# Agent attention with two layers: the last three token tiles are 416, 416 and 384 columns wide in place of 512, 512 and 192

## The chip, the cores and the metric

The kernel runs on one core of one Trainium2 chip. The metric is the device time of one execution in microseconds (us), as the median over runs. The engines of a core work side by side, each through its own queue in order: PE (TensorE) multiplies matrices, DVE (VectorE) and ACT (ScalarE) do elementwise work, POOL (GpSimd) does elementwise work on SBUF, and SP issues transfers. PE writes its results to PSUM, from which DVE and ACT read.

## The reference, cut to what matters

```python
a2k = sm(agents, k);  agent_v = a2k @ v      # softmax over 12480 keys, 49 agents
q2a = sm(q, agents);  x = q2a @ agent_v      # 12480 tokens x 128
h = x @ w_in;   g = h * (1 / (1 + exp(-h)));  x = g @ w_out     # layer 1, 2048 hidden
h = x @ w2_in;  g = h * cos(h);               out = g @ w2_out  # layer 2, 2048 hidden
```

The inputs are q, k, v (12480 x 128 each), the agents (49 x 128) and two pairs of weights. The output is 12480 x 128.

## The kernel before

The attention comes first: it leaves the softmax weights of all 12480 tokens in SBUF as `pT`, tokens along the free axis, and folds `agent_v` into the first layer's weights. It takes about the first tenth of the time and doesn't know the token tiles of the layers.

The layers run over 25 **tiles** of tokens, 24 of 512 and a last one of 192. `toks(t)` is a tile's width and `span(t)` its slice of tokens. The 2048 hidden units are cut into 16 chunks of 128. A **group** g is a quarter of a tile (`t = g // 4`, `m = g % 4`): four chunks, handled as two pairs k = 0, 1. There are NG = 100 groups. Values are split in a high part in a short format and a low part, the rest, so that three matmuls give one product; the letters h and l at the end of names say which part (`g2h`, `g2l`).

Layer 1 of a group: `L1_rest` and `L1_h` multiply into two pairs of PSUM banks (lines 543 and 555), `L1_act` applies Silu on ACT (563), `L1_hi` casts on ACT (570), `L1_lo` subtracts on DVE (578), and `L1_y` adds the product with the second weights into one bank, y1 (587, 588, 591). At a tile's end `L1_end_a` and `L1_end_b` make layer 2's input, `x2h` on ACT (608) and `x2l` on DVE (616).

Layer 2 of a group: `L2_h` (PE, 629 to 631, six matmuls a pair) gives h; `L2_n` on ACT (643) rounds h to a number of turns, `L2_r` on DVE (653) takes the turns away, `L2_cos` on ACT (662), `L2_g` on DVE (670) multiplies with h and with that frees the PSUM pair; `L2_hi` casts (679, on DVE, for some last pairs on ACT), `L2_lo` subtracts on POOL (688; the very last pair on DVE), and `L2_y` (again 587, 588, 591) adds into the one bank y2. At a tile's end `L2_end` transposes y2 on DVE (710), which frees the bank, and SP sends four transfers to the output (712).

Pairs of PSUM banks come from a pool of three (`ps`). Layer 2 runs LAG = 5 groups behind layer 1: iteration g of the last loop does layer 1 of group g and layer 2 of group q = g - 5. Up to iteration 99 the code's order is the order of each engine's queue (`manual_schedule`). At g == NG that ends (`steady.close()`): from there, where layer 1 has no more groups, a scheduler orders the queues. In the last group (`parts`) elementwise work is cut into single chunks.

Of the kernel before, what the change touches and what calls it, by code (L numbers as in the profile page):

```python
# [26 lines left out]
NWARM = 9  # L27
LATER = 150
WIDE = 512
LAG = 5  # L30
SUP = 960
LINE = 32
# [3 lines left out]
def agent_attention_moe_moe_kernel(ctx, tc, q, k, v, agents, w_in, w_out, w2_in, w2_out, out):  # L36
    nc = tc.nc
    _, N, C = q.shape
# [36 lines left out]
    def b32(ap):  # L75
        return ap.bitcast(F32)
# [367 lines left out]
    with ExitStack() as ml:  # L444
        def pool(name, bufs):
            return ml.enter_context(tc.tile_pool(name=name, bufs=bufs))
# [9 lines left out]
        g2h_p = pool("g2h", 3)  # L456
        g2l_p = pool("g2l", 3)
        o_p = pool("o", 2)
        NL = (N + WIDE - 1) // WIDE
        NG = NL * 4  # L460
        pTf = pT.rearrange("a t p s -> a (t p s)")

        def toks(t):
            return min(WIDE, N - t * WIDE)

        def span(t):
            return slice(t * WIDE, t * WIDE + toks(t))

        o1h, o1l = split["o1"]
        i2h, i2l = split["i2"]  # L470
# [8 lines left out]
        def wide(pool, tag, dt, g):  # L479
            return pool.tile([128, 2, WIDE], dt, tag=tag, name=tag)[:, :, :toks(g // 4)]  # L480

# [6 lines left out]

        avh, avl = (g1l_p.tile([128, 2, WIDE], F32R, tag="g1l", name=nm)[:, 0, :256] for nm in ("avh", "avl"))
        v.tensor_copy(out=avh, in_=pn)  # L490
# [29 lines left out]
        def in_place_low(y, cs):  # L520
            v.tensor_tensor(out=w2h[96:128, cs], in0=y[96:128], in1=b32(w2l)[96:128, cs], op=ALU.subtract)


        def L1_rest_in(t):
            if not 0 <= t < NL:
                return
            x = x3_p.tile([128, WIDE], F32R, tag="x3", name="x3")[:, :toks(t)]
            src = b32(pTf)[MORE:NA, span(t)]
            for i in range(4):
                nc.sync.dma_start(out=b32(x)[32 * i:32 * i + REST, :], in_=src)  # L530
            x3s[t] = x
# [16 lines left out]
        def L1_h(g, k):  # L548
            if not 0 <= g < NG:
                return  # L550
            t, m = g // 4, g % 4
            x = pTf[:, span(t)]
            for j in range(2):
                c = 4 * m + 2 * k + j
                nc.tensor.matmul(  # L555
                    out=h1s[g, k][:, j, :toks(t)], lhsT=w2h[:, 128 * c:128 * c + 128], rhs=x, start=False, stop=True
                )
# [35 lines left out]
        def L1_y(g, k):  # L593
            if not 0 <= g < NG:
                return
            t, m = g // 4, g % 4
            if m == 0 and k == 0:
                y1s[t] = banky("y1")[:, :toks(t)]
            gh, gl = g1s.pop((g, k))
            three(y1s[t], o1h, o1l, gh, gl, 4 * m + 2 * k)  # L600
# [34 lines left out]
        def parts(g):  # L635
            return [slice(0, 1), slice(1, 2)] if g == NG - 1 else [slice(0, 2)]
# [36 lines left out]
        def L2_hi(g, k):  # L673
# [4 lines left out]
            for p in parts(g):  # L678
                (sc.copy if k and g + LAG >= NG else v.tensor_copy)(out=gh[:, p], in_=g2s[g, k][0][:, p])  # L679
            g2s[g, k].append(gh)  # L680
# [24 lines left out]
        def L2_end(g):  # L705
            if not (0 <= g < NG and g % 4 == 3):
                return
            t = g // 4
            o = o_p.tile([128, WIDE // 32, 32], F32, tag="o", name="o")[:, :toks(t) // 32]
            v.transpose(out=o.rearrange("p b j -> p (b j)"), in_=y2s.pop(t))  # L710
            for cb in range(4):
                nc.sync.dma_start(
                    out=out[span(t), 32 * cb:32 * cb + 32].rearrange("(b i) j -> i b j", i=32),
                    in_=o[32 * cb:32 * cb + 32],
                )
# [19 lines left out]
        in_place_low(a2, q2)  # L735
        for g in range(LAG):

# [15 lines left out]
            if g == 1:  # L753
                in_place(a3, q3)
                in_place_low(a3, q3)
        for g in range(LAG, NG + LAG + 3):
            if g == NG:
                steady.close()
            q = g - LAG
            if g % 4 == 1:  # L760
# [4 lines left out]
            L1_h(g, 0)  # L765
            if g == LAG:
                L1_y(g - 1, 0)
# [56 lines left out]
```

## Time and profile before

| What | Value |
|---|---|
| median of 3 runs | 1134.94 us (1134.33 to 1134.96) |
| the profiled execution, its own time | 1131.78 us |
| its span, first to last instruction | 1130.0 us |
| busy share of the span | PE 96%, PEld (weight loads) 75%, DVE 87%, ACT 82%, POOL 48% |
| mean granted clock of PE | 0.991 of full |

Busy shares are means over the whole span. A matmul's row shows its latency, and matmuls overlap, so the distance between the starts of two that follow each other, their pitch, is what one costs on a full queue.

### The profile page before, as it was taken

Reading aid. Unit: us, or ns where it says so; the run is one execution under the profiler, and the core shown is the slowest. Engines: PE = TensorE matmul, PEld = TensorE weight load, DVE = VectorE, ACT = ScalarE, POOL = GpSimd, SP = SyncE. Lnnn points to the kernel's source line nnn. Section 1 sums busy time; section 2 is a strip of 40 time slices with the busy share of each in tenths; the row PEclk is TensorE's granted clock in tenths of the full one; section 3 lists DMA queues with packets and bytes.
Section 4 is the critical chain, followed back from the end, with each engine's and each line's share of the span. In section 5 each row is a group of like instructions: output and inputs, shape, how many; then the busy total and the mean of one; then the engine's idle time right before and its main releaser. Section 6 shows DMA issues by size and latency. Waiting matters only on the chain.

```text
span 1130.0 us, 14466 instructions
## 1 busy us (share of the span) xinstructions
PE 1084.7 (96%) x5377; PEld 851.7 (75%) x5377; DVE 988.6 (87%) x1075; ACT 923.7 (82%) x980; POOL 545.0 (48%) x291
## 2 busy tenths in 40 slices
PE   7877899999999999999999999999999999999996
PEld 5866667777777777777777777777777777777775
DVE  4899769999999999999999999999999999999884
ACT  3677698888888888888888888888888888888764
POOL 2467603554444455554444555544444555544554
PEclk9999999999999999999999999999999999999998
DMA  8898500000000000000000000000000000000000
GB/s 234 216 228 199 114 9 6 3 13 16 13 3 15 15 10 6 15 15 1 16 15 11 5 16 16 1 15 15 13 3 15 16 8 8 15 13 1 10 10 13
DMA packets 76902, 38.69 MB, mean 34 GB/s; under 512 B 52483, under 2 KB 69184, under 8 KB 76832
## 3 DMA queue, kind: packets, MB, share of 16 engines
q1 hardware_dynamic: 76832, 37.78, 14.5%
q8 instruction: 42, 0.69, 0.3%
q14 instruction: 28, 0.23, 0.1%
HBM read 27.58 MB, written 6.39 MB: 30 GB/s over the span
## 4 chain that ended last, share of the span: by engine, by line
PE 80%; DVE 8%; ACT 4%; DMA 3%; issue 3%; POOL 1%; SPq 0%; DVEq 0%; ACTq 0%; POOLq 0%
PE y L587 15%; PE y L588 15%; PE y L591 15%; PE h L555 9%; PE h L629 8%; PE h L630 8%; PE h L631 8%; PE h L543 4%; DMA wraw<-in_moe_w_in_dram 2%; DVE g L670 1%; DMA wraw<-in_moe_w_out_dram 1%; ACT g L563 1%; DVE a L248 1%; DVE m L243 1%; ACT n L662 1%
## 5 line engine op out<-in xcount | busy, mean ns | idle before, releaser
L688 POOL TENSOR_TENSOR g2l<-g,g2h 128x1024 fp32r<-128x1024 f32 (+1 forms) x200 | 466.3, 2353 | 519.4 <-DVE g1l L578 496.1
L653 DVE SCALAR_TENSOR_TENSOR n<-n,h 128x1024 f32<-128x1024 int32 (+2 forms) x202 | 239.0, 1184 | 71.7 <-ACT n L643 58.5
L643 ACT ACTIVATE n<-h,quarter 128x1024 int32<-128x1024 f32 (+2 forms) x202 | 219.6, 1088 | 91.1 <-PE h L631 91.1
L578 DVE TENSOR_TENSOR g1l<-g,g1h 128x1024 fp32r<-128x1024 f32 (+1 forms) x200 | 239.8, 1199 | 16.9 <-ACT g1h L570 7.5
L670 DVE TENSOR_TENSOR g<-n,h 128x1024 f32<-128x1024 f32 (+2 forms) x202 | 238.0, 1179 | 7.0 <-ACT n L662 3.7
L662 ACT ACTIVATE n<-n,halfpi 128x1024 f32<-128x1024 f32 (+2 forms) x202 | 226.0, 1120 | 5.6 <-DVE n L653 5.6
L563 ACT ACTIVATE g<-h 128x1024 f32<-128x1024 f32 (+1 forms) x200 | 199.5, 997 | 37.5 <-PE h L555 37.4
L570 ACT CAST g1h<-g 128x1024 fp32r<-128x1024 f32 (+1 forms) x200 | 205.0, 1025 | 3.3
L679 DVE CAST g2h<-g 128x1024 fp32r<-128x1024 f32 (+1 forms) x196 | 154.8, 790 | 7.6 <-DVE g L670 0.5
L587 PE MATMUL y<-g2h,o2h 128*128 128x512 f32 (+1 forms) x400 | 155.9, 390 | 5.1 <-DVE o L710 3.4
L587 PE MATMUL y<-g1h,o1h 128*128 128x512 f32 (+1 forms) x400 | 156.3, 392 | 0.9 <-DVE x2l L616 0.5
L629 PE MATMUL h<-x2h,i2h 128*128 128x512 f32 (+1 forms) x400 | 154.8, 387 | 1.6 <-DVE g L670 1.6
L588 PE MATMUL y<-g2h,o2l 128*128 128x512 f32 (+1 forms) x400 | 155.5, 389 | 0.0
L631 PE MATMUL h<-x2l,i2h 128*128 128x512 f32 (+1 forms) x400 | 154.4, 386 | 0.9 <-DVE x2l L616 0.9
L630 PE MATMUL h<-x2h,i2l 128*128 128x512 f32 (+1 forms) x400 | 154.4, 386 | 0.0
L588 PE MATMUL y<-g1h,o1l 128*128 128x512 f32 (+1 forms) x400 | 153.6, 385 | 0.0
L555 PE MATMUL h<-pT,w2h 128*128 128x512 f32 (+1 forms) x400 | 132.7, 413 | 0.0
L591 PE MATMUL y<-g2l,o2h 128*128 128x512 f32 (+1 forms) x400 | 122.9, 388 | 0.2 <-POOL g2l L688 0.2
L591 PE MATMUL y<-g1l,o1h 128*128 128x512 f32 (+1 forms) x400 | 121.9, 386 | 0.1
L587 PEld LDWEIGHTS y<-g1h,o1h 128*128 128x128 f32 x400 | 75.1, 188 | 24.0 <-DVE x2l L616 8.4
L587 PEld LDWEIGHTS y<-g2h,o2h 128*128 128x128 f32 x400 | 76.1, 190 | 21.3 <-DVE o L710 3.6
L555 PEld LDWEIGHTS h<-pT,w2h 128*128 128x128 f32 x400 | 67.1, 188 | 31.6 <-issue 23.6
(129 smaller groups left out, 1200.1 us busy)
## 6 DMA issues: line engine op xcount, KB each, us to landing
raw<-in_q_dram SPq DMA_DIRECT2D x13, 480.0 KB
vraw<-in_v_dram SPq DMA_DIRECT2D x13, 480.0 KB
out_dram<-o SPq DMA_DIRECT2D x96, 64.0 KB
raw<-in_k_dram SPq DMA_DIRECT2D x12, 480.0 KB
wraw<-in_moe_w_in_dram SPq DMA_DIRECT2D x8, 512.0 KB
wraw<-in_moe_w_out_dram SPq DMA_DIRECT2D x8, 512.0 KB
x<-pT SPq DMA_DIRECT2D x96, 38.0 KB
raw<-in_k_dram SPq DMA_DIRECT2D x2, 240.0 KB
```

The source lines that it names most:

```text
L555: nc.tensor.matmul(out=h1s[g, k][:, j, :toks(t)], lhsT=w2h[:, 128 * c:128 * c + 128], rhs=x, start=False, stop=True)
L578: i = v.tensor_tensor(out=gl, in0=f, in1=b32(gh), op=ALU.subtract)
L587: nc.tensor.matmul(out=y, lhsT=wh[:, c, :], rhs=gh[:, j, :], start=(c == 0), stop=False)
L588: nc.tensor.matmul(out=y, lhsT=wl[:, c, :], rhs=gh[:, j, :], start=False, stop=False)
L591: nc.tensor.matmul(out=y, lhsT=wh[:, c, :], rhs=gl[:, j, :], start=False, stop=(c == NCH - 1))
L629: nc.tensor.matmul(out=y, lhsT=i2h[:, c, :], rhs=xh, start=True, stop=False)
L630: nc.tensor.matmul(out=y, lhsT=i2l[:, c, :], rhs=xh, start=False, stop=False)
L631: nc.tensor.matmul(out=y, lhsT=i2h[:, c, :], rhs=xl, start=False, stop=True)
L653: v.scalar_tensor_tensor(out=b32(n)[:, p], in0=n[:, p], scalar=-2.0 * PI, in1=h2s[g, k][:, p], op0=ALU.mult, op1=ALU.add)
L662: sc.activation(out=r[:, p], in_=r[:, p], func=AF.Sin, bias=halfpi)
L670: v.tensor_tensor(out=f[:, p], in0=r[:, p], in1=h[:, p], op=ALU.mult)
L688: i = (v if (g, k) == (NG - 1, 1) else gp).tensor_tensor(out=gl[:, p], in0=f[:, p], in1=b32(gh)[:, p], op=ALU.subtract)
```

## The change

The widths come from a list now: 22 tiles of 512, then 416, 416 and 384, which again are 12480 tokens in 25 tiles. Number of tiles, groups and instructions per group are the same. The first changed instruction is layer 1 of group 88.

```diff
+LAST = (416, 416, 384)
...
-        NL = (N + WIDE - 1) // WIDE
+        widths = [WIDE] * ((N - sum(LAST)) // WIDE) + list(LAST)
+        begins = [sum(widths[:i]) for i in range(len(widths))]
+        assert sum(widths) == N
+        NL = len(widths)
...
         def toks(t):
-            return min(WIDE, N - t * WIDE)
+            return widths[t]

         def span(t):
-            return slice(t * WIDE, t * WIDE + toks(t))
+            return slice(begins[t], begins[t] + widths[t])
```

Up to iteration 99 the queues hold the same instructions in the same order, with other widths. Behind it the scheduler orders them anew. Line numbers of the changed kernel are higher by four there (643 is 647, 653 is 657, 662 is 666, 670 is 674, 679 is 683, 710 is 714).

ACT's queue of the last tile, groups 96 to 98, before (643 is n, 662 the cosine, 679 the cast of a pair's high part):

```order
L679 CAST g2h<-g_9819 128x1024
L643 ACTIVATE n<-h,quarter 128x2x192
L662 ACTIVATE n<-n,halfpi 128x2x192
L643 ACTIVATE n<-h,quarter 128x2x192
L662 ACTIVATE n<-n,halfpi 128x2x192
L679 CAST g2h<-g_9865 128x2x192
L643 ACTIVATE n<-h,quarter 128x2x192
L662 ACTIVATE n<-n,halfpi 128x2x192
```

And of the change, the same place:

```order
L647 ACTIVATE n<-h,quarter 128x2x384
L683 CAST g2h<-g_9819 128x2x416
L647 ACTIVATE n<-h,quarter 128x2x384
L666 ACTIVATE n<-n,halfpi 128x2x384 x2
L647 ACTIVATE n<-h,quarter 128x2x384 x2
L683 CAST g2h<-g_9865 128x2x384
L666 ACTIVATE n<-n,halfpi 128x2x384 x2
```

Before, n and cosine of a pair stand together, pair by pair, and the cast of group 96's second pair stands ahead of group 97's first n. In the change both n of a group stand together, then both cosines, and group 97's two n have moved ahead of that cast.

DVE's queue at groups 96 and 97, before (653 is r, 670 is g, 710 the transpose that frees y2 of the last tile but one):

```order
L653 SCALAR_TENSOR_TENSOR n<-n,h 128x2x192
L670 TENSOR_TENSOR g_9854<-n,h 128x2x192
L653 SCALAR_TENSOR_TENSOR n<-n,h 128x2x192
L679 CAST g2h<-g_9854 128x2x192
L670 TENSOR_TENSOR g_9865<-n,h 128x2x192
L653 SCALAR_TENSOR_TENSOR n<-n,h 128x2x192
L670 TENSOR_TENSOR g_9900<-n,h 128x2x192
L653 SCALAR_TENSOR_TENSOR n<-n,h 128x2x192
L679 CAST g2h<-g_9900 128x2x192
L710 STREAM_TRANSPOSE o<-y_9681 128x512
L670 TENSOR_TENSOR g_9918<-n,h 128x2x192
```

And of the change:

```order
L657 SCALAR_TENSOR_TENSOR n<-n,h 128x2x384 x2
L674 TENSOR_TENSOR g_9854<-n,h 128x2x384
L683 CAST g2h<-g_9854 128x2x384
L674 TENSOR_TENSOR g_9865<-n,h 128x2x384
L657 SCALAR_TENSOR_TENSOR n<-n,h 128x2x384 x2
L714 STREAM_TRANSPOSE o<-y_9681 128x416
L674 TENSOR_TENSOR g_9900<-n,h 128x2x384
L674 TENSOR_TENSOR g_9918<-n,h 128x2x384
L683 CAST g2h<-g_9900 128x2x384
```

The two r of a group now stand together, and the transpose has moved from behind group 97's first g and cast to ahead of both its g.

## Rows read from the trace of the kernel before

**Rows 1.** Windows: busy us of each engine (instructions); then granted clock, DMA share, GB/s.

```profile
981.16:1059.10 77.94, 77.94 (x353) 60.68 (x352) 71.12 (x69) 67.17 (x67) 38.24 (x16) 1.00 0.04 8
1059.10:1093.04 33.94, 32.84 (x172) 26.50 (x170) 27.81 (x33) 24.08 (x31) 19.09 (x8) 1.00 0.05 9
1093.04:1130.00 36.96, 25.80 (x145) 22.54 (x143) 20.97 (x39) 17.34 (x31) 16.74 (x12) 0.85 0.06 10
```

**Rows 2.** Timeline, PE: first L2_h matmul of iterations 88, 89, 96, 97, 98, 100 (start, us).

```profile
981.16 0.39 PE L629 MATMUL h<-x2h,i2h 128*128 128x512 f32 x1
...
991.10 0.39 PE L629 MATMUL h<-x2h,i2h 128*128 128x512 f32 x1
...
1059.10 0.39 PE L629 MATMUL h<-x2h,i2h 128*128 128x512 f32 x1
...
1068.40 0.42 PE L629 MATMUL h<-x2h,i2h 128*128 128x512 f32 x1
...
1076.96 0.42 PE L629 MATMUL h<-x2h,i2h 128*128 128x512 f32 x1
...
1093.04 0.39 PE L629 MATMUL h<-x2h,i2h 128*128 128x512 f32 x1
```

**Rows 3.** Timeline, PE: matmuls 3 places apart (512 wide), 5 apart (192 wide).

```profile
1041.81 0.39 PE L631 MATMUL h<-x2l,i2h 128*128 128x512 f32 x1
...
1042.49 0.39 PE L631 MATMUL h<-x2l,i2h 128*128 128x512 f32 x1
...
1117.75 0.27 PE L631 MATMUL h<-x2l,i2h 128*128 128x192 f32 x1
...
1118.30 0.28 PE L588 MATMUL y<-g2h,o2l 128*128 128x192 f32 x1
```

**Rows 4.** Waits of PE, 981 to 1130 us: total us, times, longest.

```profile
PE y L587 <- DVE o L710: 3.4, 1, 3.4
...
PE h L543 <- DVE g L670: 1.0, 3, 0.4
```

**Rows 5.** Timeline, ACT and DVE, iteration 97 (in brackets: idle time before, releaser).

```profile
1070.02 1.12 ACT L643 ACTIVATE n<-h,quarter 128x1024 int32<-128x1024 f32 x1 [1.79 <-PE h L631]
1071.16 1.22 DVE L653 SCALAR_TENSOR_TENSOR n<-n,h 128x1024 f32<-128x1024 int32 x1 [1.35 <-ACT n L643]
...
1072.42 1.16 ACT L662 ACTIVATE n<-n,halfpi 128x1024 f32<-128x1024 f32 x1
...
1073.68 1.22 DVE L670 TENSOR_TENSOR g<-n,h 128x1024 f32<-128x1024 f32 x1
...
1075.01 0.69 DVE L679 CAST g2h<-g 128x1024 fp32r<-128x1024 f32 x1
1075.61 1.22 DVE L670 TENSOR_TENSOR g<-n,h 128x1024 f32<-128x1024 f32 x1
```

**Rows 6.** Timeline, POOL and DVE, at the end of iteration 99's layer 1.

```profile
1093.39 2.40 POOL L688 TENSOR_TENSOR g2l<-g,g2h 128x1024 fp32r<-128x1024 f32 x1 [1.11 <-DVE g2h L679]
1094.27 1.94 DVE L578 TENSOR_TENSOR g1l<-g,g1h 128x384 fp32r<-128x384 f32 x1
```

**Rows 7.** Timeline, ACT, DVE and POOL, the last tile: group 96, last row group 99.

```profile
1103.50 0.58 ACT L643 ACTIVATE n<-h,quarter 128x384 int32<-128x384 f32 x1
1104.11 0.55 DVE L653 SCALAR_TENSOR_TENSOR n<-n,h 128x384 f32<-128x384 int32 x1 [1.66 <-ACT n L643]
1104.69 0.62 ACT L662 ACTIVATE n<-n,halfpi 128x384 f32<-128x384 f32 x1 [0.62 <-DVE n L653]
...
1106.35 0.35 DVE L679 CAST g2h<-g 128x384 fp32r<-128x384 f32 x1
...
1106.87 1.02 POOL L688 TENSOR_TENSOR g2l<-g,g2h 128x384 fp32r<-128x384 f32 x1 [0.64 <-DVE g2h L679]
...
1119.88 0.62 DVE L653 SCALAR_TENSOR_TENSOR n<-n,h 128x192 f32<-128x192 int32 x2 [1.27 <-ACT n L643]
```

**Rows 8.** Timeline, DVE: the last instruction ahead of the output's last transfers.

```profile
1125.73 0.38 DVE L710 STREAM_TRANSPOSE o<-y 128x192 f32<-128x192 f32 x1 [1.42 <-PE y L591]
```

## The prediction

> **What bounds the kernel now.** I read the windows first [rows 1]. From iteration 88 to 96, where both layers are 512 wide, PE is busy for all of 77.94 us, 9.74 us an iteration; DVE has 71.12, ACT 67.17. PE sets the pace there and DVE is close behind, 8.89 of 9.74. From 96 to 100, where layer 1 is 192 wide and layer 2 still 512, PE loses 1.1 us in the rows. From iteration 100 to the end, 36.96 us, PE is busy for 25.80 at a mean granted clock of 0.85: nothing is full there, so a chain sets the end.
>
> The timeline [rows 2] gives the iterations: 9.94 for the 88th, 9.30 for the 96th, 8.56 for the 97th, 16.08 for the 98th and 99th together. The last ones should be read against what PE has to do, for which a matmul's price is needed, its pitch: 0.68 / 3 = 0.227 us at 512 columns, 0.55 / 5 = 0.110 at 192 [rows 3]. An iteration of two 512 layers is 40 such matmuls, 9.07, and 0.67 for the four of line 543, which run side by side, and small gaps. By the same count iteration 97 is 24 of 512 and 16 of 192, 7.2 us, and some 0.5: 7.7. It took 8.56. The waits of PE [rows 4] say on whom it waits there: on g of DVE (L670), which frees the PSUM pair.
>
> That loop is in [rows 5]: from the first L2_h at 1068.40 to n 1.62 us, n to r 1.14, then DVE without a break r, r, g, cast, g until 1076.83, and the next L2_h at 1076.96. 8.56 us, all of it. So with a narrow layer 1 the loop through layer 2's elementwise work is longer than PE's work, and PE waits.
>
> **The change, up to iteration 100.** 416 and 384 columns are not in the trace. Bounds from both sides: in proportion to 512 the pitch is 0.184 and 0.170; on the line between 192 and 512 it is 0.192 and 0.180. I take 0.187 and 0.174, in between.
>
> From 88 to 96: 174 matmuls go from 512 to 416 (10 in the first iteration, 16 in each of the next four, where only layer 1 is narrower, then 28, 34 and 38, as layer 2 follows five groups behind). 174 x 0.040 = 7.0. The four of line 543, 0.05 less in each of seven iterations, 0.3. Against it, what leads iteration 96 is 384 wide in place of 192, two matmuls and line 543, 0.2. Net 7.1.
>
> From 96 to 100, before: 102 matmuls of 512 and 56 of 192, 29.3 us, with line 543 and gaps about 31; it took 33.94, so 2.9 are waits on the loop. After: 102 of 416 and 56 of 384, 19.1 + 9.7 = 28.8, and 2.2 for the rest: 31.0. The loop at 416 has six matmuls less 0.24, n 0.98, and on DVE four operations at 1.0 in place of 1.22 and a cast at 0.59, 4.75 in all: 7.2 us, under PE's 7.85. So PE doesn't wait, and 2.9 us go. Another 0.1 comes ahead of iteration 88's L2_h. By iteration 100 the changed kernel is 7.1 + 2.9 + 0.1 = 10.1 us earlier. Of that 7.1 is only put off: the columns are the same in sum, and come back in the tail.
>
> **The tail.** PE's work from iteration 100 on is 42 matmuls of the last tile but one and 102 of the last: before 42 x 0.227 + 102 x 0.110 = 20.8, after 42 x 0.187 + 102 x 0.174 = 25.6. 4.8 more, in a stretch where PE now idles for over 10. Whether it costs anything is decided by the chain, and that the scheduler has ordered anew.
>
> Before, in time from iteration 100's L2_h at 1093.04: r of group 96 starts at 11.07, r of group 99 at 26.84 [rows 7], the end is at 36.96. Three groups take 15.77, 5.26 each, though the operations are short (n 0.58, r 0.55, cosine 0.62, g 0.55): ACT's queue takes them pair by pair, so every step waits for the one before on the other engine, and the transpose (L710) that frees y2 stands so late on DVE that PE waits for it for 3.4 us [rows 4].
>
> After, widths of 768 a pair, by the lines between the 1024 and 384 forms [rows 5, 7]: n 0.90, r and g 0.95, cosine 0.94, cast on DVE 0.55; POOL's L2_lo 1.85, between 2.40 [rows 6] and 1.02. PE has 30 matmuls ahead of group 96 (24 x 0.187 + 6 x 0.174 = 5.5), waits for x2l until about 6.6, and four more and n bring r of group 96 to 8.5. Per group DVE has r, r, g, cast, g, 4.35 us, and n and cosine of both pairs stand ahead of them on ACT in the new order. I add 0.75 per group for the pair's n that comes late, because PE has to get a free PSUM pair from g, and for the cast: where POOL works, a DVE operation with SBUF operands alone is held, as the subtraction that took 1.94 and ended just after POOL did [rows 6]. In the middle group the transpose's 0.6 takes that place. 5.1 + 4.9 + 5.1, r of group 99 at 23.6. From there four r in halves (2.2), the cosines to 27.6, g to 28.6, the last two subtractions held by POOL until 29.4 and done at 30.5, two matmuls, at half clock perhaps, and the transpose, 32.4. From the end of the transpose to the span's end was 1130.0 - 1126.1 = 3.9 [rows 8]; so 36.3. The tail is 0.7 shorter, with 4.8 more work in it. Its ends: 33, if neither late n nor POOL costs anything (three groups at 4.35, and 1 us from the last), and about 47 for the order of before at the new widths (below).
>
> **The sum.** 10.1 + 0.7 = 10.8. The profiled execution took 1131.78 (span 1130.0, and 1.78 around it), so 1121.0; the median of the runs is 3.16 above the profiled one, which I carry over: 1134.94 - 10.8 = 1124.1.
>
> **A rule against it.** The two widths in [rows 3] differ by 117 ns in pitch for 320 columns, most of what columns alone would make at the 2.4 GHz level. The Trainium skill, "TensorE: Matmul & The Clock Gate", section "Back-to-back issue gap", has for streams of weight load and matmul about 81 ns at 128 columns and 131 at 512, so that 384 columns less save only 50 ns. As an estimate from that page, 416 would save 13 ns in place of 40, and the 7.1 put off would be about 2.3, with nearly 10 us instead of 4.8 coming back in the tail: no gain at all. This trace disagrees in both figures, 227 ns where the page has 131, and in the slope, almost three times the page's.
>
> **Rivals.** (1) *DVE becomes the bound in the mixed stretch.* For it: DVE is at 91% and only the subtraction of layer 1 (L578) shrinks while layer 2 is 512. If DVE's waits of 0.85 an iteration stay, five iterations take 8.49 + 0.85 = 9.34 in place of 9.06 and the six after it some 0.3 more as well: 3.2 us, 1127.3. Against it: the loop of [rows 5] has room, 8.56 against 9.06.
>
> (2) *The tail runs as the one before did*, each pair's n, r, cosine and g one behind the other. Four steps at 768 are 3.74 against 2.30 before, so a group takes 5.26 x 1.63 = 8.6, and three groups 10.6 more than I have. That is the whole gain; with the last group's matmuls at half clock behind such idle time, 2 us, it ends slower, at 1136.5. It decides from a period of 8 us. Against it: the new order on both queues.
>
> (3) *The pitch hardly falls between 512 and 384 columns*, the drop to 192 being at the narrow end. At 0.227 for both the gain to iteration 100 is lost, 276 x 0.040 + 58 x 0.053 = 14.1, and the tail's 144 matmuls take 32.6 with some 4 us on its end: 1134.94 - 10.8 + 14.1 + 3.7 = 1142. Against it only the slope in [rows 3].
>
> **How the numbers follow.** My forecast 0.80, with its own range 1120.5 to 1127 (the pitch's bounds are -1 and +2.5 us, the tail's late n and POOL -2 and +2). Rival 1 0.10, rival 2 0.06, rival 3 0.04. The range of 8 in 10 reaches to rival 1 and beyond the pitch's good end: 1119.5 to 1129. Under 0.2%, 2.3 us, a measurement of this kernel tells no difference. Faster: forecast and rival 1, 0.90; rivals 2 and 3 mostly slower, 0.07, or halfway, 0.03.
>
> **What would show it.** Starts of L2_h 1.0 to 1.1 us closer in iterations with a pitch of 0.187 at 416; no wait on L670 from 96 to 99, and iterations 97 and 98 at 7.85; iteration 100's L2_h near 1083; r of group 96 to group 99 in 15 us; y2's transpose no longer a wait of 3.4; granted clock above 0.85 in the tail. It is wrong if the pitch stays over 0.20, if L670 appears among PE's waits again, or if the tail from iteration 100 is over 40 us.

## The result and the profile after

The changed kernel took 1122.2 us (median of 4 runs, 1120.5 to 1123.1) against 1134.6 of before on the same chip, a ratio of 0.9897 with a 95% interval of 0.9871 to 0.9923. Forecast were 1124.1 us, and 1119.5 to 1129 with room for the rivals.

Its profiled execution has a span of 1121.1 us, 8.9 less than before's 1130.0. The layers gained more than that: in this execution the attention, whose code is the same, ended 1.9 us later (the first matmul behind it starts at 141.04 in place of 139.13), and so iteration 88's first L2_h starts at 982.87 in place of 981.16. From there on the two traces are compared. The windows of the change, cut at the first L2_h of iterations 88, 96 and 100 as in [rows 1] (us; then busy us of PE, weight loads, DVE, ACT and POOL with instructions; granted clock):

```profile
982.87:1054.15 71.28, 71.19 (x353) 60.42 (x352) 65.46 (x69) 60.02 (x67) 36.55 (x16) 1.00 0.05 10
1054.15:1085.13 30.98, 30.98 (x171) 29.20 (x171) 27.75 (x34) 26.81 (x32) 16.18 (x9) 1.00 0.04 8
1085.13:1121.10 35.97, 28.27 (x145) 25.06 (x144) 27.75 (x38) 22.46 (x31) 20.55 (x12) 0.99 0.07 12
```

| Stretch | before | after, forecast | after |
|---|---|---|---|
| iteration 88 to 96 | 77.94 | 70.8 | 71.28 |
| 96 to 100 | 33.94 | 31.0 | 30.98 |
| 100 to the end | 36.96 | 36.3 | 35.97 |

In sum 148.84 became 138.23, 10.6 us less. PE, which lost 1.1 us between 96 and 100, is busy without a gap there. In the tail it is busy for 28.27 in place of 25.80, at a granted clock of 0.99 in place of 0.85.

The pitch of the new widths, from PE's timeline (start, duration): matmuls 11 places apart at 416 columns, 5 apart at 384.

```profile
1085.13 0.35 PE L633 MATMUL h<-x2h,i2h 128*128 128x416 f32 x1
...
1087.21 0.35 PE L635 MATMUL h<-x2l,i2h 128*128 128x416 f32 x1
...
1092.23 0.33 PE L635 MATMUL h<-x2l,i2h 128*128 128x384 f32 x1
...
1093.10 0.33 PE L635 MATMUL h<-x2l,i2h 128*128 128x384 f32 x1
```

2.08 / 11 = 0.189 and 0.87 / 5 = 0.174. PE's longest waits from iteration 88 on, to be held against [rows 4]:

```profile
PE y L595 <- POOL g2l L692: 1.9, 4, 0.8
PE y L591 <- DVE o L714: 0.9, 1, 0.9
```

No wait on g is left, the one on the transpose went from 3.4 to 0.9, and near the end PE waits for POOL's subtractions, 1.9 us in four waits. DVE's timeline at the start of groups 96 and 99, and the last transpose:

```profile
1093.60 0.95 DVE L657 SCALAR_TENSOR_TENSOR n<-n,h 128x768 f32<-128x768 int32 x1 [0.63 <-ACT n L647]
...
1108.52 1.00 DVE L657 SCALAR_TENSOR_TENSOR n<-n,h 128x384 f32<-128x384 int32 x2
...
1116.42 0.58 DVE L714 STREAM_TRANSPOSE o<-y 128x384 f32<-128x384 f32 x1 [0.71 <-PE y L595]
```

Counted from iteration 100's L2_h, r of group 96 starts at 8.47, r of group 99 at 23.39, and the end is at 35.97. Before it was 11.07, 26.84 and 36.96 [rows 7]. Twice as many columns go through the three groups in 14.9 us in place of 15.8.

### The profile page after: what moved, and what is told of

The parts are those of the page before. It is cut to its first block, busy times and chain, and to the rows that moved or that the text cites. A ratio compares the mean times of both kernels' runs of the same rounds, so it can differ in the third digit from the quotient of the medians.

```text
span 1121.1 us, 14463 instructions
## 1 busy us (share of the span) xinstructions
PE 1083.5 (97%) x5377; PEld 862.0 (77%) x5377; DVE 988.1 (88%) x1075; ACT 924.1 (82%) x980; POOL 544.0 (49%) x291
## 4 chain that ended last, share of the span: by engine, by line
PE 84%; DMA 4%; DVE 4%; ACT 3%; issue 3%; POOL 2%; SPq 0%; POOLq 0%; ACTq 0%; DVEq 0%
PE y L591 15%; PE y L595 15%; PE y L592 15%; PE h L559 9%; PE h L633 8%; PE h L635 8%; PE h L634 8%; PE h L547 4%; DMA wraw<-in_moe_w_in_dram 2%; ACT g L567 1%; DMA wraw<-in_moe_w_out_dram 1%; DMA raw<-in_q_dram 1%; POOL g2l L692 1%; PE h L313 1%; PE y L359 1%
## 5 line engine op out<-in xcount | busy, mean ns | idle before, releaser
L692 POOL TENSOR_TENSOR g2l<-g,g2h 128x1024 fp32r<-128x1024 f32 (+2 forms) x200 | 465.4, 2349 | 509.4 <-DVE g1l L582 499.6
L657 DVE SCALAR_TENSOR_TENSOR n<-n,h 128x1024 f32<-128x1024 int32 (+3 forms) x202 | 239.0, 1184 | 64.2 <-ACT n L647 51.3
L647 ACT ACTIVATE n<-h,quarter 128x1024 int32<-128x1024 f32 (+3 forms) x202 | 219.7, 1088 | 89.4 <-PE h L635 89.3
L582 DVE TENSOR_TENSOR g1l<-g,g1h 128x1024 fp32r<-128x1024 f32 (+2 forms) x200 | 239.6, 1198 | 16.6 <-ACT g1h L574 10.2
L674 DVE TENSOR_TENSOR g<-n,h 128x1024 f32<-128x1024 f32 (+3 forms) x202 | 238.0, 1179 | 3.5 <-ACT n L666 0.2
L567 ACT ACTIVATE g<-h 128x1024 f32<-128x1024 f32 (+2 forms) x200 | 199.5, 997 | 36.3 <-PE h L559 36.2
L666 ACT ACTIVATE n<-n,halfpi 128x1024 f32<-128x1024 f32 (+3 forms) x202 | 225.7, 1119 | 0.8 <-DVE n L657 0.8
L574 ACT CAST g1h<-g 128x1024 fp32r<-128x1024 f32 (+2 forms) x200 | 204.9, 1025 | 3.3
L683 DVE CAST g2h<-g 128x1024 fp32r<-128x1024 f32 (+2 forms) x196 | 155.0, 791 | 7.8 <-DVE g L674 0.5
L591 PE MATMUL y<-g1h,o1h 128*128 128x512 f32 (+2 forms) x400 | 156.5, 391 | 0.9 <-DVE x2l L620 0.4
```

Of the source, the lines that this page charges most:

```text
L582: i = v.tensor_tensor(out=gl, in0=f, in1=b32(gh), op=ALU.subtract)
L591: nc.tensor.matmul(out=y, lhsT=wh[:, c, :], rhs=gh[:, j, :], start=(c == 0), stop=False)
L657: v.scalar_tensor_tensor(out=b32(n)[:, p], in0=n[:, p], scalar=-2.0 * PI, in1=h2s[g, k][:, p], op0=ALU.mult, op1=ALU.add)
L666: sc.activation(out=r[:, p], in_=r[:, p], func=AF.Sin, bias=halfpi)
L674: v.tensor_tensor(out=f[:, p], in0=r[:, p], in1=h[:, p], op=ALU.mult)
L692: i = (v if (g, k) == (NG - 1, 1) else gp).tensor_tensor(out=gl[:, p], in0=f[:, p], in1=b32(gh)[:, p], op=ALU.subtract)
```

## The experiments

My account has two parts: up to iteration 100 widths alone decide, through PE's work and a loop through layer 2's elementwise work; behind it the order of the queues decides. The main rival: the order is of no account, the widths do it all. Widths and order change together in this change, so the first two experiments part them. Below, "the stretch" is iterations 88 to 99 and "the tail" all from iteration 100's first L2_h on. The tail is written out by hand there, as a list of steps that is run through under `manual_schedule` up to the end; the step "L2_n,-4,0" stands for L2_n(NG - 4, 0):

```diff
-        for g in range(LAG, NG + LAG + 3):
-            if g == NG:
-                steady.close()
+        for g in range(LAG, NG):
...
+        for step in TAIL.split():
+            ...
+        steady.close()
```

**Old widths, new order.**

> Widths of before (512, 512, 192), but from iteration 100 on the queues stand in the order of the changed kernel, written out by hand. My theory (the tail is a chain whose length the order decides): up to iteration 100's first L2_h nothing changes (111.9 us from iteration 88); the tail shrinks from 36.96 to about 30.5 us, r of group 96 to r of group 99 from 15.8 to about 10, since n, r, cosine and g of a group's two pairs overlap; the 3.4 us wait for the transpose is gone. Median about 1128, ratio 0.9945. Rival (the order hardly matters, the tail is PE's work with a fixed end): tail 36 to 37.5, ratio 1.000.

Measured: ratio 0.9951 (0.9932 to 0.9969), median 1127.05. The windows, cut at iterations 88 and 100:

```profile
984.46:1096.33 111.87, 110.77 (x524) 87.25 (x523) 98.94 (x101) 91.19 (x98) 57.35 (x24) 1.00 0.05 8
1096.33:1126.50 30.17, 23.04 (x145) 19.70 (x143) 21.62 (x39) 16.97 (x31) 16.72 (x12) 0.98 0.07 13
```

The stretch is that of before, the tail 6.8 us shorter with the same widths. r of group 96 to r of group 99 took 11.7 us, more than the 10 I gave it: about half of the excess is a cast in group 96 that took 1.21 us, in place of 0.35, while POOL worked. PE's longest wait is 1.2, and the granted clock falls only behind the last matmul, so its mean is 0.98. The rival is out.

**New widths, old order.**

> Widths of the change (416, 416, 384), but from iteration 100 on the queues stand in the order of before, written out by hand. My theory (rival 2 of the prediction put to the test): iteration 88 to 100 stays at 102.3 us, the tail goes to about 46 us, three groups at 8.6 us each in place of 5.0; median about 1132, ratio 0.998, nearly the whole gain lost. Rival (the order hardly matters): tail 36 to 37.5, ratio 0.990 as the change.

Measured: ratio 1.0004 (0.9988 to 1.0019).

```profile
980.36:1082.65 102.29, 102.20 (x523) 89.67 (x522) 93.41 (x102) 86.84 (x98) 52.80 (x25) 1.00 0.05 9
1082.65:1129.50 46.85, 31.62 (x145) 28.65 (x144) 27.53 (x38) 23.00 (x31) 20.43 (x12) 0.82 0.05 9
```

With the order of before the whole gain is gone, as rival 2 of the prediction had it. The stretch keeps its 9.6 us, the tail takes them back. In DVE's timeline one sees the chain: an operation waits for ACT, and ACT in turn waits for it (the cosine for r, 1.02 us). Group 97's first pair:

```profile
1099.94 0.95 DVE L669 SCALAR_TENSOR_TENSOR n<-n,h 128x768 f32<-128x768 int32 x1 [1.76 <-ACT n L659]
1101.96 0.95 DVE L686 TENSOR_TENSOR g<-n,h 128x768 f32<-128x768 f32 x1 [1.07 <-ACT n L678]
```

Groups 96 to 99 took 23.7 us, 7.9 each, where I gave 8.6. PE waits for the transpose for 5.2 us, and its clock is 0.82 in the tail. The order of before by hand at the old widths was not run, so what the hand-written form itself costs in that order isn't shown.

**Control: new widths, new order by hand.**

> Control for the two kernels with a tail written out by hand: widths 416, 416, 384 and the changed kernel's order by hand. If writing the order out costs nothing of itself, tail 35 to 37 us and ratio 0.9885 to 0.992, as the change. If the hand-written form itself costs or gains (the scheduler's finer interleaving of matmuls matters), the tail is off by over 1 us.

Measured: ratio 0.9909 (0.9881 to 0.9937), within the interval of the change.

```profile
1083.26:1121.00 37.74, 29.03 (x145) 26.01 (x144) 27.75 (x38) 22.47 (x31) 20.50 (x12) 0.90 0.07 11
```

The hand-written tail is longer than the 35 to 37 us expected, and 1.8 us longer than the scheduler's. Its steps are whole, so that it can't put a pair's matmuls between those of another, and the wait for the transpose is 1.5 in place of 0.9. From r of group 96 to r of group 99 the difference is 0.6 us (15.54 against 14.92). Another 1.1 lies between there and the last matmul's end, 8.96 us at a granted clock of 0.85 against 7.87 at 1.00. So compare by hand with by hand: at the new widths the order is worth 46.85 - 37.74 = 9.1 us.

Of these, 8.1 lie between r of group 96 and r of group 99 (23.66 against 15.54), 2.7 for each of the three groups. The first of them takes 7.63 against 4.87, though in the old order its last step, group 97's n, starts at 1099.01, ahead of PE's wait for the transpose, which starts at 1099.62. So in that group the place of the transpose isn't the cause. Whether the pairs' order alone is, or the place of ACT's casts with it, no experiment parts.

**The cast behind g.** This asks whether the loop of [rows 5] is what holds iterations 96 to 98 of before.

```diff
-            L2_hi(q - 1, 0)
+            if not 96 < g < NG:
+                L2_hi(q - 1, 0)
...
             L2_g(q - 1, 1)
+            if 96 < g < NG:
+                L2_hi(q - 1, 0)
```

> The kernel before, but in the code of iterations 97, 98 and 99 the cast of the first pair (L2_hi) stands behind g of the second pair (L2_g) on DVE. My theory (the loop L2_h, n, r, r, g, cast, g, L2_h sets iterations 96 to 98 of before): each of these three is about 0.6 us shorter, 9.30 to 8.7, 8.56 to 7.97, 8.89 to 8.3, 1.8 us in all; PE's wait for L670 in them falls from 1.0 us to near 0; tail unchanged; ratio 0.9985. Rival (PE's narrow matmuls, held at the weight load's 0.11 us, set these iterations): they stay as they are.

Measured: iterations 96 to 98 took 9.29, 8.49 and 8.62 us, 0.35 less in sum, and the ratio is 0.999 (0.9974 to 1.0006). The loop as I had drawn it doesn't carry the time. In iteration 97 g of the second pair ended 7.86 us behind L2_h in place of 8.43, but PE still waited 0.42 at line 543 for g of the first pair, and what PE has behind that wait fills the time until L2_h.

The tail, expected unchanged, took 35.30 us in place of 36.96, though its queues hold the same instructions in the same order. Over half of that lies between r of group 97 and r of group 98, where the granted clock differs, first of before, then of this kernel (windows as in [rows 1]):

```profile
1108.85:1114.98 6.13, 2.85 (x14) 2.85 (x15) 2.91 (x7) 2.79 (x5) 2.57 (x3) 0.78 0.25 43
```

```profile
1112.99:1118.23 5.24, 1.96 (x16) 1.97 (x17) 2.91 (x6) 2.79 (x5) 2.21 (x3) 0.96 0.16 29
```

**The second pair of L1_rest later.** `L1_rest` is given the numbers of the matmuls of line 543 that it is to issue.

```diff
-            L1_rest(g)
+            L1_rest(g, (0, 1) if 96 < g < NG else (0, 1, 2, 3))
...
             L2_y(q - 2, 0)
+            if 96 < g < NG:
+                L1_rest(g, (2, 3))
```

> The kernel before, but in the code of iterations 97 to 99 the two matmuls of L1_rest for the second pair (the ones that wait for g of the first pair, L670) stand behind L2_y(q-2, 0) on PE, two places later. After the cast alone failed to shorten the loop, my theory is that there are two loops of equal length, 8.56 us: L2_h to g of the first pair to line 543 and the matmuls behind it, and L2_h to g of the second pair to the next L2_h. Then this edit alone frees only the first: iterations 96 to 98 stay at 9.3, 8.56 and 8.9 within 0.1, PE's wait moves from line 543 to L2_h (line 629). Rival (only the loop through line 543 binds): 97 falls to 8.0.

Measured: 9.22, 8.56 and 9.14, ratio 1.0001 (0.9986 to 1.0017). Iteration 97 stays exactly, as two equal loops have it. Iteration 98 became 0.25 longer, because the order now makes line 543 wait for L2_y, which waits 0.6 us for the transpose there.

**Both edits.**

> Both edits: the second pair's L1_rest behind L2_y(q-2, 0) and the cast behind g. Theory of two equal loops: now both are shorter, the second by what the cast alone showed in g (it ended 7.86 us behind L2_h): iteration 97 at 8.0, 96 at 8.7 and 98 at 8.4, 1.6 us less in sum for the three; ratio 0.9985. Rival (PE's narrow matmuls at 0.11 us set these iterations): no change, 9.3, 8.56, 8.9.

Measured: 9.16, 8.24 and 9.14, ratio 1.0002 (0.9986 to 1.0018). Iteration 97 is 0.32 shorter, with either edit alone 0.07 and 0. So two loops there are. The other two fell short of what was expected, 9.16 for 8.7 and 9.14 for 8.4; the 98th holds the wait of 0.6 for the transpose again. And in the 97th 8.0 was not reached; the windows of iteration 97 say why, first of before, then of this kernel (us, PE busy):

```profile
1068.40:1076.96 8.56, 8.16 (x45) 6.66 (x45) 6.94 (x9) 6.11 (x8) 4.77 (x2) 1.00 0.00 0
```

```profile
1073.61:1081.85 8.24, 8.24 (x46) 6.65 (x44) 6.69 (x9) 6.01 (x8) 4.77 (x2) 1.00 0.00 0
```

At 8.24 PE has no gap left. PE's own work in such an iteration is 8.1 to 8.2 us, not the 7.7 that I had counted from the two pitches. The starts of its matmuls say where a part of the rest goes. Of before, behind a block of 192 columns, the first two of 512 start 0.25 apart:

```profile
1072.07 0.41 PE L587 MATMUL y<-g2h,o2h 128*128 128x512 f32 x1
1072.32 0.40 PE L588 MATMUL y<-g2h,o2l 128*128 128x512 f32 x1
```

The tail's queues are those of before in all three kernels edited ahead of it. Their tails took 35.30, 36.47 and 36.30 us, before's 36.96. The clock fell to half 18.8, 19.2, 19.7 and 20.7 us behind iteration 100's L2_h (both edits, before, L1_rest alone, cast alone), and r of group 97 to r of group 98 took 6.22, 6.13, 5.66 and 5.24: the later the fall, the shorter. So a tail read from one trace is uncertain by up to 1.7 us.

**Another split, 480, 416 and 320.**

> The last three tiles 480, 416 and 320 wide, all else as in the change. My theory (with the loop shorter than PE's work and the new order, the time is PE's work and about 10 us in which it has none, so that the split of the last 1216 columns hardly matters): iteration 88 to 100 about 104.8, tail about 33.5, sum 138.3 as in the change (138.2); ratio 0.989 to 0.991. Rival (the last tile's width sets the end, narrower is better as long as PE does not wait): 2 us better than the change, ratio 0.988. Rival (the loop binds again, 320 beside 480): iterations 96 to 98 over 8.8 us, ratio 0.992.

Measured: ratio 0.9928 (0.9909 to 0.9946), median 1124.26.

```profile
983.21:1088.51 105.30, 105.17 (x524) 88.53 (x523) 95.35 (x102) 88.39 (x98) 54.62 (x24) 1.00 0.05 9
1088.51:1122.40 33.89, 26.27 (x145) 23.51 (x143) 25.79 (x38) 20.59 (x31) 18.98 (x12) 0.90 0.07 12
```

In sum these are 139.19 us, 1.0 us more than the change; the forecast for the parts was 104.8 and 33.5. The ratio missed the 0.989 to 0.991 expected, though its interval overlaps the change's. The stretch is 3.0 us longer and the tail 2.1 shorter. The loop doesn't bind: iteration 96 took 8.80, 97 and 98 took 7.85 and 7.66, and PE has no wait in them.

**The narrow tile first.**

```diff
-        widths = [WIDE] * ((N - sum(LAST)) // WIDE) + list(LAST)
+        widths = [FIRST] + [WIDE] * ((N - FIRST) // WIDE)    # FIRST = 192
```

> The tile of 192 is the first and not the last, the 24 others are 512; the scheduler orders the tail. My theory (a narrow tile costs where a narrow layer 1 stands beside a wide layer 2, and where a wide tile fills the tail it fills time in which PE idles): no iteration from 88 to 99 over 9.95 us, no waits for L670, the tail about 43 us (r of group 96 to r of group 99 18.7), iteration 100 some 14 us earlier than before; ratio about 0.993. Rival (a wide last tile makes a tail so long that it is slower than 192 at the end): tail over 50 us, ratio 1.00 or more.

Measured: in the trace no iteration from 88 to 99 took over 9.93 us, there is no wait on g, the tail is 44.4 us, and r of group 96 to r of group 99 took 18.1; iteration 100 starts 12.6 us earlier, not 14. The profiled run took 1126.73, about 2 us more than expected. But ten runs spread from 1122.4 to 1134.1, and the ratio is 0.9979 (0.9956 to 1.0002), a miss. Hence a second trace of the same kernel:

> The kernel with the narrow tile first once more, for its trace: its timed runs spread from 1122 to 1134 us while its profiled run took 1126.7. If the layers vary, the stretch from iteration 88 to the end differs from 160.8 us by over 1 us; if what lies ahead of them varies (the attention, with its transfers), that stretch is 160.8 within 0.5 and the start of iteration 88 moves.

Measured: 1130.84 us, iteration 88 to the end 160.8 as in the first trace. So the layers' end doesn't differ between the two. The attention ended alike too: the first matmul of line 507, which opens the layers, starts at 141.33 and 141.50. The 4.2 us lie between, ahead of the first L2_h, which starts at 164.13 and 168.30; windows from 150 to 170 us of the first and of the second trace:

```profile
150.00:170.00 20.00, 18.54 (x127) 14.95 (x124) 11.69 (x20) 17.95 (x30) 0.00 (x0) 1.00 0.03 10
```

```profile
150.00:170.00 20.00, 20.00 (x106) 17.35 (x107) 8.89 (x14) 14.73 (x25) 0.00 (x0) 0.66 0.03 10
```

It is the same code at a granted clock of 1.00 and 0.66: 127 matmuls against 106. That tells these two executions apart. Why the clock falls in one of them is open, and whether it explains the other runs isn't shown.

No experiment points to a version that beats the change: PE has 0.1 us of gaps from iteration 88 to 100, and in the tail 4.7 of its 7.7 idle us lie behind the last matmul, in the transpose and the output.

## Why the prediction was right

*To iteration 100.* Forecast were 10.1 us, measured 9.6 (111.88 to 102.26) and 0.15 ahead of it. The pitches held: 0.189 and 0.174 for 0.187 and 0.174. The two iterations with x2l, 88 and 92, cost 9.56 and 9.50 where a free PE would need 9.1, a little more than allowed.

*One term of it was wrong in size.* I put 2.9 us of iterations 96 to 100 down to waits on the loop. Their sum, 33.94 to 30.98, came out to 0.1 us, but not their cause; that was luck. In the rows PE idles 1.1 us [rows 1], of which 1.0 at line 543 [rows 4], and with both loops loosened iteration 97 won 0.32 and not 0.86. The rest is PE itself: an iteration of 24 wide and 16 narrow matmuls takes it 8.1 to 8.2 us. Behind a block of narrow ones the wide ones start up to 0.26 apart, in place of 0.227, for a while, which is 0.2 us in an iteration, and line 543, split by the wait, costs 0.3 a pair and 0.1 on either side. A pitch read from rows of one width doesn't show that. And there was not one loop but two of 8.56 us; I followed the one through g of the second pair, though the wait that I cited sat on the other.

*The tail.* Forecast 36.3, measured 35.97; r of group 96 at 8.5 and 8.47, r of group 99 at 23.6 and 23.39; the end from there, 12.7 and 12.6. The 0.75 a group that I added was right in size and only in part in its cause. In groups 96 and 98 the second pair's n came late, and DVE waited 0.62 and 0.43 for it. It stood behind a cast on ACT, while its matmuls had ended 0.8 and 0.4 us before it; I had put that down to a PSUM pair. A cast on DVE met POOL's work in group 98 alone, and took 1.00 us there against 0.56 in group 96. That the new order makes room for 4.8 us more of PE's work was the step on which the gain hung, and the pair of experiments by hand shows it: the same widths with the old order end 9.1 us later than with the new one.

*The total.* Forecast were 10.8 us. The traces give 10.8 as well, 10.6 and the 0.15 ahead, and that close a meeting is luck: 10.1 for 9.8 up to iteration 100 and 0.7 for 1.0 in the tail cancel, and the tail of before varies by more. The medians differ by 12.4, with an interval from 8.7 to 14.6.

*The sum by cause.* Tails are 36.96 and 30.17 us at the old widths in the old and the new order, 46.85 and 35.97 at the new ones; 30.17 and 46.85 are by hand. New widths win 9.6 us ahead of the tail in either order. In the old order the tail takes 9.9 of it back; in the new one 5.8, or 7.6 by hand (37.74 - 30.17). So of 10.6 us the new order is worth some 6.8 at the old widths, and the widths 2 to 4 once the order is right. Since the tail of before was 35.3 to 37.0 us in its four traces, 6.8 may be as little as 5.1; the medians of the first experiment differ by 5.7. The prediction had put 10.1 and 0.7 by place, which is right, but a reader would take it for the widths' gain.

*The rivals.* DVE did not become the bound: 9.07 to 9.10 for 9.06 in the mixed iterations. Rival 2 is what the same widths do in the old order; its time should read 1136.7 by its own terms, not 1136.5. The pitch fell as columns do: the estimate from the Trainium skill ("TensorE: Matmul & The Clock Gate", section "Back-to-back issue gap") would have had 416 at 13 ns less than 512; it was 38.

## What to carry to other kernels

A change of tile widths at the end also changes what a scheduler does with the drain; start there, and write one of the two out by hand before giving the widths the credit. In a drain, try operations that go to and fro between two engines pair beside pair in both queues, so that one engine works on one pair while the other has its sibling. Here the new order as a whole was worth 5 to 7 us at the old widths and 9 at the new. Moving work into a tail in which the bound engine idles isn't free: of the 9.6 us won ahead of it, the tail took 9.9 back in the old order and 5.8 to 7.6 in the new one. So the move alone won nothing, and with the new order 10.6 us were won in all.

## What the runs showed of the hardware that was not expected

The granted clock of one stretch can differ between executions of one program: 1.00 and 0.66 over 20 us in the kernel with the narrow tile first, 4.2 us apart at iteration 88, with the same end to the attention within 0.2 us. The clock of the tail differs too, and there it costs time: four traces have the tail of before with the same queues, and its step from r of group 97 to r of group 98 took 6.22 us where the clock fell to half earliest and 5.24 where it fell latest. In these it fell during the wait of 3.4 us or within 1.6 us behind it, and with a wait of 5.2 us during that. In the change and in the first experiment, with waits of 0.9 and 1.2 at most, it fell only behind the last matmul. But it fell ahead of the last matmul in the split of 480, 416 and 320 as well, where the longest wait is 0.8, so that the length of a wait alone doesn't tell.
